# Block loads, and transposes by DMA in place of TensorE, in a fused window-attention and SwiGLU kernel

## The chip, the cores and the metric

The kernel runs on one core of a Trainium2 chip. The metric is the device time of one execution in microseconds (us). Before the change it is 247.0 us (median of three, 246.82 to 247.25). The profile is of one execution whose span is 245.4 us; all times within the kernel count from the start of that span.

## What is computed

Causal attention over a window of 128 positions plus 4 sink positions, for 4 batches, 8 heads, 768 positions and head size 64; its output, laid out as 3072 tokens of 512, goes through an RMS norm and a SwiGLU feed-forward of width 1536.

```python
keep = (pos < 4) | ((rel >= 0) & (rel < 128))     # rel = query - key
a = softmax(where(keep, q @ k.T / sqrt(64), -1e9));  x = (a @ v) as [3072, 512]
xn = x / sqrt(mean(x * x) + 1e-6) * rms_g
out = (silu(xn @ w_gate) * (xn @ w_val)) @ w_out
```

## The kernel before

**Blocks and groups.** The 3072 tokens are 24 blocks `g` of 128, six to a batch (`NT` = 6). The feed-forward takes four blocks at a time, so there are six groups `G` (group 2 is blocks 8 to 11). A block goes through a load of q, k and v (`unit_load`, L126, issued on GpSimd, with a cast to bf16), a transpose of q and k (`unit_t`, L265), scores and exponentials (`unit_s`, L399), attention times values (`unit_attend`, L488), the norm (`unit_rms`, `unit_xr`, L531 and L571) and a transpose of the normed block (`unit_x`, L602). A group then runs 12 feature tiles of gate and value products (L642) and four output products of 12 matmuls (L702).

**Two ways to transpose.** q and k of blocks 12 and up, but not of block 18, are transposed by a DMA that SyncE issues (L271); the others by TensorE (L245) with a copy by ScalarE (L279). The normed x of blocks 12 and up is transposed by DMA (L589), that of earlier blocks by TensorE (L612) with a copy by ScalarE (L621).

**Masks and sinks.** From block 8 on, GpSimd masks the exponentials (L388, L393), except in blocks that begin a batch; `pv` (L467, L471) reads them. GpSimd's queue therefore holds both loads and masks, in the order of the program. Once per batch, ScalarE copies the sink keys from the transposed k of the batch's first block (L290, `ksk`; the batches begin at blocks 0, 6, 12, 18).

**What sets the order.** A list of slots, worked off between the parts of a group (`run`, L740), writes out the order of TensorE, SyncE and GpSimd. In groups 1 to 5 parts 0 to 23 are the gate and value halves of the 12 feature tiles and parts 24 to 35 the output products; `step` (L718) puts the attention of a block at the parts in `AT` (L737) and pops its loads from `LOADS` (L738). The first group's second half has a list of its own (`FIRST`, L790), in which parts 12 to 23 are output products. The order on ScalarE and VectorE is left to a scheduler there: an instruction of theirs that waits holds all behind it.

**Buffers.** All products of TensorE rotate through eight PSUM tiles of one bank each (`psum`, L86), so a new product waits until the reader of an earlier one in its bank is done. Each GpSimd load also waits for the landing of the load eight before it. The output tiles `osb` (L707) have three buffers.

Of the kernel before, what the change touches and what calls it, by code (L numbers as in the profile page):

```python
# [15 lines left out]
P = 128  # L16
# [12 lines left out]
def kernel(  # L29
# [21 lines left out]
    NT = S // P  # L51
# [4 lines left out]
    GB = 4  # L56
# [7 lines left out]
    RMS_EPS = 1e-6 * RSQRT_SCALE ** 2  # L64
    MS_SCALE = RSQRT_SCALE / math.sqrt(DM)
    DMA_T_FROM = 12
    DMA_X_FROM = 12
    LD = 15
    FA = FTN
    POOL_MASK_FROM = 8  # L70
# [55 lines left out]
    def unit_load(g):  # L126
        if g not in QS:
            load_q(g)
            load_k(g)
        load_v(g)  # L130
# [112 lines left out]
    def transposes(ps, src, c0):  # L243
        for hp in range(HP):
            nc.tensor.transpose(  # L245
                out=ps[:, c0 + hp * P:c0 + (hp + 1) * P],
                in_=src[:, 2 * hp:2 * hp + 2, :], identity=ident,
            )
# [11 lines left out]
        )  # L260

    def by_dma(g):
        return g >= DMA_T_FROM and g != 3 * NT

    def unit_t(g):  # L265
        b, t = divmod(g, NT)
        if t == 0:
            QKT[b] = qkt.tile([P, 2, HP, S], BF16, name="qkT")
        if by_dma(g):
            for i, src in enumerate((QS.pop(g), KS_.pop(g))):  # L270
                nc.sync.dma_start_transpose(  # L271
                    out=QKT[b][:, i, :, t * P:(t + 1) * P],
                    in_=src.rearrange("p h d -> p (h d)"),
                )
            return
        ps = psum.tile([P, 512], FP32, name="pqk", tag="b1").bitcast(BF16)
        transposes(ps, QS.pop(g), 0)
        transposes(ps, KS_.pop(g), HP * P)
        nc.scalar.copy(  # L279
            out=QKT[b].rearrange("p i h s -> p (i h) s")[:, :, t * P:(t + 1) * P],  # L280
            in_=ps.rearrange("p (x c) -> p x c", c=P),
        )
# [205 lines left out]
    def unit_attend(g):  # L488

        if g % NT >= 2:  # L490
            unit_sink_av(g)
        for u in range(2):
            unit_av(g, u)
# [77 lines left out]
    def unit_xr(g):  # L571
# [14 lines left out]
        if tb == 0:  # L586
            XNT[G] = xtpool.tile([P, KTN, GN], BF16, name="xnt")
        if g >= DMA_X_FROM:
            nc.sync.dma_start_transpose(  # L589
# [5 lines left out]
    def unit_scale(gs):  # L595

        with tc.issue_after(LAST[0]):
            unit_rms(gs)
            for g in gs:
                unit_xr(g)  # L600

    def unit_x(g):  # L602
        if g >= DMA_X_FROM:
            return
        G, tb = divmod(g, GB)
        xr = XR.pop(g)
        n = KTN // 2 if g < 2 else KTN
        for k0 in range(0, KTN, n):
            ps = psum.tile([P, 512], FP32, name="pxt", tag="b1").bitcast(BF16)
            for i in range(n):  # L610
                kt = k0 + i
                nc.tensor.transpose(  # L612
                    out=ps[:, i * P:(i + 1) * P], in_=xr[:, kt * P:(kt + 1) * P],
                    identity=ident,
                )
            dest = XNT[G][:, k0:k0 + n, tb * P:(tb + 1) * P]
            src = ps[:, 0:n * P].rearrange("p (k c) -> p k c", c=P)
            if g == 2 * GB - 1:
                nc.vector.tensor_copy(out=dest, in_=src)
            elif g >= 2:  # L620
                nc.scalar.copy(out=dest, in_=src)  # L621
            elif k0 > 0:
                nc.vector.tensor_tensor(
                    out=dest, in0=src,
                    in1=gt[:, k0:k0 + n].unsqueeze(2).to_broadcast((P, n, P)),
                    op=ALU.mult,
                )
            else:
                for i in range(n):
                    nc.scalar.mul(dest[:, i, :], src[:, i, :], gt[:, k0 + i:k0 + i + 1])  # L630
# [17 lines left out]
    def parts_f(G, fts, cols, between=None):  # L648
        st = {}
        n = len(fts)  # L650

        def gate():
            st["pg"] = mms("pg", wg, G, fts, cols)
            st["th"] = spool.tile([P, 512], BF16, name="th")
            nc.scalar.activation(out=st["th"], in_=st["pg"], func=ACT.Tanh, scale=0.5)  # L655

        def val():
            pvl = mms("pvl", wv, G, fts, cols)
            p1 = spool.tile([P, 512], BF16, name="p1")
            nc.vector.scalar_tensor_tensor(  # L660
                out=p1, in0=st["th"], scalar=1.0, in1=st["pg"],
                op0=ALU.add, op1=ALU.mult,
            )
            if between:
                between()
            key = (G, fts[0] // 2)
            if key not in HT:
                HT[key] = hpool.tile([P, 2, GN], BF16, name="hT")
            i = fts[0] % 2
            LAST[0] = nc.vector.tensor_tensor(  # L670
                out=HT[key][:, i:i + n, cols],
                in0=p1.rearrange("p (n c) -> p n c", n=n),
                in1=pvl.rearrange("p (n c) -> p n c", n=n), op=ALU.mult,
            ).ins

        return [gate, val]
# [18 lines left out]
    def parts_o(G, tb):  # L695
        st = {}

        def part(i):
            if i == 0:
                st["po"] = psum.tile([P, 512], FP32, name="po", tag="b1")  # L700
            for ft in range(4 * i, 4 * i + 4):
                nc.tensor.matmul(  # L702
                    out=st["po"], lhsT=HT[(G, ft // 2)][:, ft % 2, tb * P:(tb + 1) * P],
                    rhs=wo[:, ft, :], start=(ft == 0), stop=(ft == FTN - 1),
                )
            if 4 * i + 4 == FTN:
                osb = opool.tile([P, DM], FP32, name="osb")  # L707

                nc.scalar.mul(osb, st["po"], 0.5)  # L709
                row = (G * GB + tb) * P  # L710
                n = P // 2 if G == 4 and tb < 2 else P
                for r in range(0, P, n):
                    nc.sync.dma_start(out=out[row + r:row + r + n, :], in_=osb[r:r + n])

        return [lambda i=i: part(i) for i in range(FTN // 4)]


    def step(g, p):  # L718

        b, t = divmod(g, NT)  # L720
        slots = [[] for _ in range(7)]
        if g < NB:
            if t in (2, 4):
                slots[0].append(lambda: unit_sink_scores(b, t))
            slots[0].append(lambda: unit_s(g))
            if t == 1:
                slots[2].append(lambda: unit_sink(b))
        if g <= NB:
            slots[0].append(lambda: unit_attend(g - 1))
        for n in (g + 2, g + 3):  # L730
            if n < NB and n not in (10, 12, 13) and by_dma(n) == (n == g + 3):
                slots[4].append(lambda n=n: unit_t(n))
        for n in LOADS.pop(0) if LOADS else ():
            slots[1].append(lambda n=n: unit_load(n))
        return [(p + i, u) for i, us in enumerate(slots) for u in us]

    AT = [(0, 8, 14, 20, 28), (0, 10, 18, 27)]  # L737
    LOADS = [(14, 15), (16, 17), (18, 19), (20, 21), (22, 23)]  # L738

    def run(parts, slots):  # L740

        slots = sorted(slots, key=lambda e: e[0])
        for s, f in enumerate(parts):
            while slots and slots[0][0] <= s:
                slots.pop(0)[1]()
            f()
        while slots:
            slots.pop(0)[1]()

    with tc.manual_schedule(engines=MANUAL_ALL):  # L750
# [60 lines left out]
        (19, lambda: unit_x(5)),  # L811
        (19, lambda: unit_t(9)),
        (20, lambda: unit_attend(7)),
        (18, lambda: unit_t(10)),
        (24, lambda: unit_t(12)),
        (24, lambda: unit_t(13)),
        (22, lambda: unit_sink_scores(1, 2)),
# [28 lines left out]
        ])  # L846
    with tc.manual_schedule(engines=MANUAL):

        for g in range(2 * GB + 2, 2 * GB + 6):
            FIRST.append((3 * g - 28, lambda g=g: unit_load(g)))  # L850
        for G in range(NG):
            if G == 0:
                parts, slots = fb, FIRST
            else:
                parts, slots = [], []
                for ft in range(FTN):
                    parts += parts_f(G, (ft,), slice(0, GN))
                g0, n = (9, 5) if G == 1 else (4 * G + 6, 4)
                for g in range(g0, min(g0 + n, NB + 1)):
                    slots += step(g, AT[G > 1][g - g0])  # L860
                if G + 2 <= NG:
                    gs = GROUP[GB * (G + 1)]
                    slots.append((25, lambda gs=gs: unit_scale(gs)))
                    for i, g in enumerate(gs):
                        slots.append((30 + i, lambda g=g: unit_x(g)))
            for tb in range(GB):
                parts += (parts_last if G * GB + tb == NB - 1 else parts_o)(G, tb)
            run(parts, slots)
# [33 lines left out]
```

The softmax here doesn't subtract the row's maximum and nothing guards it: scores larger than these inputs give would overflow.

## Time and profile before

| Engine | busy us | share of the span |
|---|---|---|
| TensorE, matmuls (PE) | 239.0 | 97% |
| TensorE, weight loads (PEld) | 127.8 | 52% |
| VectorE (DVE) | 163.2 | 66% |
| ScalarE (ACT) | 143.8 | 59% |
| GpSimd (POOL) | 105.3 | 43% |

The profile gives, besides these sums, a row for each group of like instructions and a timeline for each engine with start, length and, in brackets, how long the engine stood idle before and what ended that. SyncE and the DMA queues have rows for each issue, and the landing of each transfer is known. A long busy share says that an engine always has something in it; whether a change pays is read from who waits for whom in the stage that the change touches. Group 1 runs from about 66.7 to 105.5 us, group 2 from 105.5 to about 142, group 3 from there to about 178.

### The profile page before, as it was taken

What the parts mean: (1) busy time and instruction counts of PE and PEld (TensorE: products, weight loads), DVE (VectorE), ACT (ScalarE), POOL (GpSimd) and SP (SyncE); (2) the same over time, 40 slices, a digit from 0 to 9 for tenths busy, and PEclk for the clock granted to TensorE, in tenths of its full rate; (3) what the DMA queues carried; (4) which work ended last, traced back from release to release, by engine and by line L of the source; (5) the groups of instructions that cost most, each with busy time, mean ns of one, the idle gap of its engine ahead of it and who ended that gap; (6) DMA issues with size and microseconds to landing.
All of it is one profiled execution on the core that took longest, in us unless ns stands there. A gap on an engine that the chain in (4) does not pass through costs nothing.

```text
span 245.4 us, 4880 instructions
## 1 busy us (share of the span) xinstructions
PE 239.0 (97%) x1809; PEld 127.8 (52%) x1834; DVE 163.2 (66%) x367; ACT 143.8 (59%) x334; POOL 105.3 (43%) x141
## 2 busy tenths in 40 slices
PE   7999999999999999999999999999999999999995
PEld 3656888855544444554454454444444444444443
DVE  4557897878657889149778278769067885187800
ACT  2869648899977574785583385674475341323212
POOL 8967676598598997951232001233231000000000
PEclk9999999999999999999999999999999999999999
DMA  9999999999989999999001674001610002700012
GB/s 128 146 173 190 193 156 188 186 155 192 184 108 129 159 152 151 129 165 136 0 3 21 169 155 87 0 4 23 192 45 0 0 3 57 191 9 3 0 74 98
DMA packets 104937, 25.48 MB, mean 104 GB/s; under 512 B 94033, under 2 KB 101969, under 8 KB 104914
## 3 DMA queue, kind: packets, MB, share of 16 engines
q0 software_dynamic: 80704, 13.90, 75.8%
q1 hardware_dynamic: 23026, 10.95, 20.4%
q10 hardware_dynamic: 1184, 0.33, 0.6%
q8 instruction: 14, 0.23, 0.4%
q14 instruction: 9, 0.07, 0.1%
HBM read 28.31 MB, written 6.29 MB: 141 GB/s over the span
## 4 chain that ended last, share of the span: by engine, by line
PE 87%; DVE 5%; issue 3%; ACT 3%; POOL 1%; ACTq 0%; POOLq 0%
PE pg L642 24%; PE pvl L642 24%; PE po L702 22%; PE pT L411 4%; PE pv L467 2%; PE pv L471 2%; PE pw L332 2%; PE pqk L245 2%; PE po L684 1%; ACT sq L519 1%; DVE hT L670 1%; PE pv L453 1%; ACT et L420 1%; PE pT L357 1%; DVE x L508 1%
## 5 line engine op out<-in xcount | busy, mean ns | idle before, releaser
L642 PE MATMUL pg<-xnt,wg 128*128 128x512 bf16 (+1 forms) x326 | 73.6, 348 | 0.7
L642 PE MATMUL pvl<-xnt,wv 128*128 128x512 bf16 (+1 forms) x331 | 73.6, 348 | 0.2
L655 ACT ACTIVATE th<-pg 128x512 bf16<-128x512 f32 x72 | 43.2, 602 | 43.0 <-PE pg L642 41.8
L660 DVE SCALAR_TENSOR_TENSOR p<-th,pg 128x512 bf16<-128x512 bf16 x72 | 49.2, 684 | 28.1 <-ACT th L655 27.7
L702 PE MATMUL po<-wo,hT 128*128 128x512 bf16 x267 | 62.2, 379 | 0.4
L670 DVE TENSOR_TENSOR hT<-p,pvl 128x512 bf16<-128x512 bf16 x72 | 49.4, 687 | 7.8 <-PE pvl L642 1.1
L388 POOL TENSOR_SCALAR_AFFINE_SELECT et<-et 128x512 bf16<-128x512 bf16 x28 | 19.2, 694 | 70.3 <-ACT et L420 70.2
L642 PEld LDWEIGHTS <-wv 128*128 128x128 bf16 x336 | 32.4, 98 | 29.6 <-issue 0.2
L642 PEld LDWEIGHTS <-wg 128*128 128x128 bf16 x336 | 31.5, 98 | 26.5 <-issue 1.0
L420 ACT ACTIVATE et<-pT 128x512 bf16<-128x512 f32 x76 | 39.5, 609 | 4.0 <-PE pT L411 3.9
L702 PEld LDWEIGHTS <-hT 128*128 128x128 bf16 x276 | 26.1, 98 | 29.1 <-issue 0.2
L709 ACT ACTIVATE osb<-po 128x512 f32<-128x512 f32 x23 | 13.8, 598 | 31.8 <-PE po L702 27.4
L519 ACT ACTIVATE sq<-x 128x256 bf16<-128x256 bf16 x48 | 20.3, 426 | 7.9 <-DVE x L508 7.2
L121 POOL DMA_DIRECT2D v<-in_v_dram x24 | 21.8, 911 | 3.1 <-DMA wo<-in_moe_w_out_dram 2.0
L108 POOL DMA_DIRECT2D qs<-in_q_dram x23 | 20.9, 911 | 4.9 <-DMA wo<-in_moe_w_out_dram 3.0
L108 POOL DMA_DIRECT2D ks<-in_k_dram x23 | 20.9, 907 | 2.4 <-DMA wv<-in_moe_w_val_dram 0.7
L503 DVE RECIPROCAL rden<-pv 128x4 f32<-128x4 f32 x48 | 7.6, 171 | 20.3 <-PE pv L471 20.2
L508 DVE TENSOR_TENSOR x<-pv,rden 128x256 bf16<-128x256 f32 x48 | 19.9, 422 | 1.0
L582 DVE SCALAR_TENSOR_TENSOR xr<-x,y,gb 128x512 bf16<-128x512 bf16 x22 | 16.9, 814 | 0.3
L393 POOL TENSOR_SCALAR_AFFINE_SELECT et<-et 128x512 bf16<-128x512 bf16 x22 | 14.8, 673 | 0.0
L471 PE MATMUL pv<-v,et 128*128 128x65 bf16 x168 | 12.7, 194 | 0.3 <-POOL et L388 0.2
L411 PE MATMUL pT<-qkT 64*128 64x256 bf16 (+1 forms) x168 | 12.0, 262 | 0.0
(82 smaller groups left out, 192.3 us busy)
## 6 DMA issues: line engine op xcount, KB each, us to landing
out_dram<-osb SPq DMA_DIRECT2D x21, 256.0 KB, 2.4
v<-in_v_dram POOLq DMA_DIRECT2D x24, 128.0 KB, 7.2
qs<-in_q_dram POOLq DMA_DIRECT2D x23, 128.0 KB, 6.8
ks<-in_k_dram POOLq DMA_DIRECT2D x23, 128.0 KB, 6.9
wg<-in_moe_w_gate_dram POOLq DMA_DIRECT2D x6, 256.0 KB, 8.6
wv<-in_moe_w_val_dram POOLq DMA_DIRECT2D x6, 256.0 KB, 8.7
wo<-in_moe_w_out_dram POOLq DMA_DIRECT2D x2, 768.0 KB, 10.4
out_dram<-osb SPq DMA_DIRECT2D x4, 128.0 KB, 2.4
```

The costliest lines, as they stand in the source:

```text
L108: nc.gpsimd.dma_start(out=tl, in_=src[b, :, t * P:(t + 1) * P, :].rearrange("h t d -> t h d"),)
L121: nc.gpsimd.dma_start(out=V16[b][:, t, :, 0:D], in_=v[b, :, t * P:(t + 1) * P, :].rearrange("h t d -> t h d"),)
L388: nc.gpsimd.affine_select(out=ev[:, :, 0, :], in_=ev[:, :, 0, :], compare_op=ALU.is_ge, fill=0.0, base=0, pattern=[[0, x], [1, P]], channe ...
L411: nc.tensor.matmul(out=banks[u][hi][:, j * w:(j + 1) * w], lhsT=QKT[b][pr, 1, hp, t * P:(t + 1) * P], rhs=QKT[b][pr, 0, hp, t * P:t * P + ...
L420: nc.scalar.activation(out=et[:, hi].rearrange("p j n c -> p (j n c)"), in_=banks[u][hi], func=ACT.Exp, scale=inv_sqrt_d,)
L508: nc.vector.tensor_tensor(out=X16[g][:, heads_of(g, u), :], in0=pvv[:, :, 0:D], in1=RDEN.pop((g, u)).unsqueeze(2).to_broadcast((P, 4, D)), ...
L519: nc.scalar.activation(out=sq, in_=xh, func=ACT.Square, scale=MS_SCALE, accum_out=MS[g - i][:, i, u:u + 1],)
L642: nc.tensor.matmul(out=ps[:, i * n:(i + 1) * n], lhsT=w_sb[:, kt, ft * P:(ft + 1) * P], rhs=XNT[G][:, kt, cols], start=(kt == 0), stop=(kt ...
L655: nc.scalar.activation(out=st["th"], in_=st["pg"], func=ACT.Tanh, scale=0.5)
L660: nc.vector.scalar_tensor_tensor(out=p1, in0=st["th"], scalar=1.0, in1=st["pg"], op0=ALU.add, op1=ALU.mult,)
L670: LAST[0] = nc.vector.tensor_tensor(out=HT[key][:, i:i + n, cols], in0=p1.rearrange("p (n c) -> p n c", n=n), in1=pvl.rearrange("p (n c) - ...
L702: nc.tensor.matmul(out=st["po"], lhsT=HT[(G, ft // 2)][:, ft % 2, tb * P:(tb + 1) * P], rhs=wo[:, ft, :], start=(ft == 0), stop=(ft == FTN ...
```

## The change

It takes TensorE's transposes away for x of blocks 8 to 11 and for q and k of block 18 and gives them to the DMA, in the way the later blocks already have them. The loads of blocks 14 and 15 move from group 1 into the output parts of group 0, so the later loads each come a step earlier or, for 20 to 23, behind the x of the second group, so as to leave the DMA free when the x of blocks 8 to 11 is to be transposed. The transpose of block 10 stands a few instructions later, and the outputs of blocks 18 and 19 are written in halves as those of 16 and 17 are.

```diff
-    DMA_X_FROM = 12
+    DMA_X_FROM = 8
...
     def by_dma(g):
-        return g >= DMA_T_FROM and g != 3 * NT
+        return g >= DMA_T_FROM
...
-                n = P // 2 if G == 4 and tb < 2 else P
+                n = P // 2 if G == 4 else P
...
-    LOADS = [(14, 15), (16, 17), (18, 19), (20, 21), (22, 23)]
+    LOADS = [(16, 17), (18, 19), (), (), (20, 21), (22, 23)]
...
-        (18, lambda: unit_t(10)),
+        (19, lambda: unit_t(10)),
...
-        for g in range(2 * GB + 2, 2 * GB + 6):
+        for g in range(2 * GB + 2, 2 * GB + 8):
             FIRST.append((3 * g - 28, lambda g=g: unit_load(g)))
```

## Prediction

> **What bounds the kernel now.** I read the busy sums first, then TensorE's waits by stage, then the timelines of GpSimd, ScalarE and SyncE around the edits, and last the landing times of the DMAs.
>
> From the page, the busy sums and the chain that ended last, by engine:
>
> ```profile
> PE 239.0 (97%) x1809; PEld 127.8 (52%) x1834; DVE 163.2 (66%) x367; ACT 143.8 (59%) x334; POOL 105.3 (43%) x141
> ...
> PE 87%; DVE 5%; issue 3%; ACT 3%; POOL 1%; ACTq 0%; POOLq 0%
> ```
>
> TensorE is nearly always busy, and from 66.7 us on its recorded waits for other engines add up to a few tenths. So work taken off it is saved in full, and any new wait of it is lost in full: nothing later catches it up. The change is a balance of these two.
>
> GpSimd's timeline where group 0 becomes group 1, and TensorE's row that waits for it (start, length, engine, line, tiles; in brackets the idle time before and its releaser):
>
> ```profile
> 59.59 0.91 POOL L121 DMA_DIRECT2D v<-in_v_dram  x1
> 64.17 1.05 POOL L388 TENSOR_SCALAR_AFFINE_SELECT et<-et 128x512 bf16<-128x512 bf16 x1 [3.67 <-ACT et L420]
> 65.18 0.63 POOL L393 TENSOR_SCALAR_AFFINE_SELECT et<-et 128x512 bf16<-128x512 bf16 x1
> 65.77 0.63 POOL L388 TENSOR_SCALAR_AFFINE_SELECT et<-et 128x512 bf16<-128x512 bf16 x1
> ...
> 66.45 0.20 PE L471 MATMUL pv<-v,et 128*128 128x65 bf16 x1 [0.19 <-POOL et L388]
> ```
>
> GpSimd ends its last load at 60.5 and idles 3.67 us until block 8's exponentials come. TensorE takes the third mask the moment it ends: these masks have no slack.
>
> ScalarE's timeline early in group 1, and the landing times (min/median/max) of the two transposes of block 12 in front of it:
>
> ```profile
> 70.38 0.41 ACT L290 COPY ksk<-qkT 64x16 bf16<-64x16 bf16 x2 [1.11 <-DMA qkT<-ks]
> 70.82 0.60 ACT L655 ACTIVATE th<-pg 128x512 bf16<-128x512 f32 x1
> ...
> DMA to landing us min/median/max: 2.4/2.5/2.5
> ```
>
> The sink copy of batch 2 waits for that DMA, and the `th` behind it waits too, though its `pg` is ready at about 69.4. SyncE's last transposes before group 3, and the landings of the four around them:
>
> ```profile
> 108.60 1.30 SPq L271 DMA_TRANSPOSE qkT<-qs  x1
> 109.99 3.04 SPq L271 DMA_TRANSPOSE qkT<-ks  x1
> ...
> DMA to landing us min/median/max: 5.9/7.3/8.9
> ```
>
> So a transpose lands in about 2.4 us alone and in 5.9 to 8.9 us (5.5 at the least in 73 to 81 us) while loads are in flight.
>
> **What the Trainium skill says.** "DMA: Bandwidth & Descriptors", section "Issuing engines are not separate DMA queues", says that DMAs from SyncE, ScalarE and GpSimd share 16 DMA engines and interleave; the two landing times above agree. "TensorE: Matmul & The Clock Gate", in its opening table, calls the queues of ScalarE, VectorE and GpSimd strict FIFOs; the `th` held at 70.82 agrees. "PSUM — Partial Sum Buffer", "Specifications (TRN2)", gives 8 banks per partition: a late reader can be outrun by eight products, not more. The trace agrees: the two L453 matmuls of block 9, whose second waits for the `p` of feature tile 3, take 0.45 us at 74.80 against 0.27 us elsewhere. "TensorE: Matmul & The Clock Gate", "Part 4: PE-mode transpose", gives about 275 ns for a transpose in a kernel; here four of them move the next row on from 98.11 to 98.33, so I take 0.055 us each.
>
> **What is removed.** Blocks 8 to 11: 16 transposes, 16 x 0.055 = 0.9 us of TensorE; block 18: 8 x 0.055 = 0.45 us. Together -1.35 us. Six ScalarE copies go as well (four of 0.6 us, one of 1.0); nothing on TensorE waits for ScalarE's time there, so nothing. Moving block 10's transpose hides its 0.3 us wait for `ks` at 57.18, but only until TensorE waits for the masks at 66, so nothing either. The halved outputs of blocks 18 and 19: ScalarE waits 3.21 us for an output buffer at 212.69 and TensorE runs on; nothing.
>
> **Step 1, masks of block 8.** In the changed kernel's order the six loads of blocks 14 and 15 stand ahead of the masks of block 8. Six at the loads' pace of 0.87 us from 60.5 end at 65.7; the wait of each for the landing of the load eight earlier (7.0 us) adds up to 0.2. The masks start near 65.85 in place of 64.17, and the third ends 1.65 us later. Queued behind it are TensorE's `pv` of block 8 and all of group 1: +1.65 us. Bounds: 1.4 to 2.0.
>
> **Step 2, sink copy of batch 2.** SyncE issues block 12's transposes at 66.5 and 67.9 as before, but now the loads of 14 and 15 are in flight. The nearest case is block 14's pair of before, issued at 74.25 and 76.26 just as six loads had been issued: it landed with the last of these, at 81.7 and 81.95. The last load now is issued at 65.0 and lands some 7 us later, at 72; I put the k transpose at 73.0 (70.4 if alone, 75 with 7.5 us). ScalarE's queue holds `th` of tile 1 behind it. From the copy to the end of `p` of tile 3, on which the second L453 waits, it takes 74.93 - 70.38 = 4.55 us, all in VectorE's rows without a gap, and before the change this was already just the time that TensorE came. So TensorE's delay is now the copy's: 73.0 - 70.4 = 2.6 us in all, of which step 1 is a part. Call this s = 2.6; bounds 1.65 to 4.1. All of group 1 moves by s.
>
> **Step 3, x of blocks 8 to 11.** The `xr` come at 96.0 to 98.4 (+s). Four issues of 1.3 us end at 101.2 + s, and the last lands by 102.3 (2.4 us) to 104.3 (4.4, as the transpose at 69.23 with a load beside it). TensorE comes to group 2 at 105.5 - 0.9 = 104.6 + s. Hidden: nothing. The output of block 4 now goes behind them, at 101.3 + s, and the fourth output buffer waits for its landing, at 104 to 106 + s; `pg` of group 2 needs that bank at 104.6, which could cost up to 1.5 us, but step 4 takes it up.
>
> **Step 4, sink copy of batch 3.** Block 18's transposes come on SyncE behind four x, four outputs and the transposes of 16 and 17: 96.0 + 10 x 1.3 + 4 x 0.4 puts the k one at 109.4 + s, within 0.6 us of the pair shown above (109.99), with as many loads (20, 21) issued from 100 to 105.3 as 22 and 23 were then. That one landed at 115.84, so I take 116 + s; alone it would be 111.8. ScalarE's order has this copy behind the second `th` of group 2, near 108, and before the third. Behind it wait `th`, `p` and `hT` of tile 2 and after. By the eight-bank rotation the scores of block 15 need `p` of tile 2, and the next `pg` (feature tile 5) needs `p` of tile 4. With the steps seen in group 1 `p` of tile 4 ends 4.6 us after the transpose lands: 120.6 + s, where before that `pg` started at 115.41. Cost 5.2 us, in which the 0.9 us saved before it and the bank of step 3 are already contained. If alone: 111.8 + 4.6 - 115.4 = 1.0 us.
>
> **Sum.** 247.0 + 2.6 + 5.2 - 0.45 (block 18, later in group 2) = 254.35; I say 254.3 us.
>
> **Rivals.**
> - The transposes land as if alone. For it: the loads of 18 and 19 are over long before group 2, and a queue of its own might get its turn. Against: no transpose beside loads took under 4.4 us. Then 247.0 + 1.65 + 1.0 - 0.45 = 249.2 us. 20%.
> - Faster: the masks and the sink copies are hidden after all, and only TensorE's saving is left, with the 0.3 us for block 10: 247.0 - 1.35 - 0.3 = 245.35 us. For it: TensorE at 97%. Against: the mask wait at 66.45 and both copies in ScalarE's order. 8%.
> - No change: step 1 costs 1.65 us, the rest is hidden: 247.0 + 1.65 - 1.35 - 0.3 = 247.0 us. 5%.
> - Worse: block 18's transposes also wait for the loads of 22 and 23 (issued from 108.8 + s) and land 8.9 us after an issue 1 us later, at 119.2 + s, with s = 4.1: 247.0 + 4.1 + (119.2 + 4.6 - 115.4) - 0.45 = 259.05 us. 9%.
>
> **How the numbers follow.** The forecast has the rest, 58%, and reaches from about 252 (copies landing 1 us sooner in each step) to 257. The range 249.0 to 258.0 takes in the first rival and leaves out faster, no change and most of worse, some 20%. Chances: faster 0.08, same 0.05, slower 0.87.
>
> **What would show it.** Step 1: the first L388 after the loads starts near 65.9 with no idle time before it, and TensorE's `pv` waits 1.5 us or more for it. Step 2: the first L290 with a DMA as releaser waits 2 to 4 us. Step 3: `pg` of group 2 not released by a DMA. Step 4: an idle time of some 7 us ahead of the second L290, and TensorE's largest gap of the kernel at block 15. Were that copy's wait under 3 us, the forecast would be wrong; were the masks of block 8 on time, step 1 would be.

## The result, and the profile after

The changed kernel takes 265.8 us (median of four, 265.15 to 266.55) against 247.1 us for the kernel before: a ratio of 1.0758 (95% interval 1.0727 to 1.0789). The forecast was 254.3 us with a range up to 258.0: the sign was right, and the loss was more than twice the one forecast. The spans of the two profiled executions, 263.9 and 245.4 us, differ by 18.5 us, and these are followed below.

From the page of the changed kernel: the busy sums, the granted TensorE clock in 40 slices of the span (tenths of full speed, 9 for 90% or more), and the chain that ended last, by engine:

```profile
PE 241.8 (92%) x1785; PEld 127.8 (48%) x1810; DVE 162.2 (61%) x367; ACT 141.2 (54%) x329; POOL 105.0 (40%) x141
...
PEclk9999999999999999997579999999999999999999
...
PE 81%; DMA 8%; DVE 4%; ACT 3%; issue 2%; SPq 0%; DVEq 0%; ACTq 0%
```

TensorE has 24 matmul rows less and is yet busy for 2.8 us more, because some ran at a lower clock: that is the 7 and the 5 near slice 20. DMA, which before had no share in the chain that ended last, now has 8%, and TensorE's share of the span has gone from 97% to 92%.

**Step 1.** GpSimd's timeline of the changed kernel at the end of its loads, and TensorE's row that waits for it:

```profile
63.70 0.88 POOL L108 DMA_DIRECT2D qs<-in_q_dram  x1 [0.75 <-DVE y L547]
64.86 0.88 POOL L108 DMA_DIRECT2D ks<-in_k_dram  x1 [0.28 <-DVE xr L582]
65.72 0.88 POOL L121 DMA_DIRECT2D v<-in_v_dram  x1
66.60 0.66 POOL L388 TENSOR_SCALAR_AFFINE_SELECT et<-et 128x512 bf16<-128x512 bf16 x1
...
68.47 0.20 PE L471 MATMUL pv<-v,et 128*128 128x65 bf16 x1 [0.75 <-POOL et L388]
```

The masks (L388) start with no idle time, right behind the last load of block 15. TensorE takes the third one at 68.47 in place of 66.45: 2.0 us.

**Steps 2 to 4.** ScalarE's timeline: the two sink copies, and between them the last output copy of group 1:

```profile
74.78 0.41 ACT L290 COPY ksk<-qkT 64x16 bf16<-64x16 bf16 x2 [4.02 <-DMA qkT<-ks]
...
109.25 0.60 ACT L709 ACTIVATE osb<-po 128x512 f32<-128x512 f32 x1 [3.35 <-PE pv L471]
...
127.47 0.42 ACT L290 COPY ksk<-qkT 64x16 bf16<-64x16 bf16 x2 [13.63 <-DMA qkT<-ks]
```

The copy of batch 2 waits 4.0 us for a DMA (1.1 before) and that of batch 3 waits 13.6 us (none before). For the output copy at 109.25 the profile names TensorE as the releaser, but the output write issued at 105.36 lands at 109.14, just before the copy starts: it waited for the output buffer. SyncE's timeline has the transposes of block 18 and the two output writes that x pushed back:

```profile
100.14 5.12 SPq L589 DMA_TRANSPOSE xnt<-xr  x4
105.36 1.00 SPq L713 DMA_DIRECT2D out_dram<-osb  x2
...
114.64 2.19 SPq L271 DMA_TRANSPOSE qkT<-qs  x1
116.92 3.35 SPq L271 DMA_TRANSPOSE qkT<-ks  x1
```

In its records the k transpose, issued at 116.92, lands at 127.44: 10.5 us later. TensorE's timeline shows what the two waits of group 2 become there:

```profile
109.90 1.02 PE L642 MATMUL pg<-xnt,wg 128*128 128x512 bf16 x3 [0.69 <-ACT osb L709]
...
129.28 0.37 PE L411 MATMUL pT<-qkT 64*128 64x256 bf16 x1 [10.26 <-DVE p L660]
...
132.64 0.61 PE L642 MATMUL pg<-xnt,wg 128*128 128x512 bf16 x1
...
135.86 1.03 PE L642 MATMUL pg<-xnt,wg 128*128 128x512 bf16 x4
```

The last two rows are the gate matmuls of feature tiles 5 and 6. In the kernel before these were:

```profile
115.41 1.02 PE L642 MATMUL pg<-xnt,wg 128*128 128x512 bf16 x3
...
117.14 1.03 PE L642 MATMUL pg<-xnt,wg 128*128 128x512 bf16 x4
```

Last, windows of 2 us: busy time of TensorE's matmuls, its weight loads, VectorE, ScalarE and GpSimd with their counts, then the granted clock as a share of full speed, the DMA column and GB/s:

```profile
120.00:122.00 2.00, 0.00 (x0) 0.00 (x0) 0.00 (x0) 0.00 (x0) 0.00 (x0) 1.00 1.70 135
122.00:124.00 2.00, 0.00 (x0) 0.00 (x0) 0.00 (x0) 0.00 (x0) 0.00 (x0) 0.51 2.24 151
...
132.00:134.00 2.00, 1.78 (x18) 1.17 (x18) 1.72 (x6) 0.51 (x2) 0.93 (x2) 0.50 0.00 0
134.00:136.00 2.00, 2.00 (x7) 0.74 (x6) 0.69 (x1) 0.99 (x3) 0.00 (x0) 0.58 0.00 0
136.00:138.00 2.00, 2.00 (x11) 0.88 (x9) 1.07 (x2) 0.60 (x1) 0.00 (x0) 1.00 0.00 0
```

None of these engines does anything from 120 to 126 us (the window of 124 to 126, not shown, is as empty as the one before it); during it the clock falls to half, and it stays there until about 135.7, well after the matmuls are back.

The shift against the kernel before can be read off the first gate matmul (`pg`, L642) of each stage: 4.4 us at feature tile 4 of group 1 (80.08 against 75.68), 4.4 at the first of group 2 (109.90 against 105.53), 17.2 at feature tile 5 of group 2 (132.64 against 115.41), 18.7 at the tile behind it (135.86 against 117.14), and 18.5 at the end.

### The profile page after: what moved, and what is told of

Same layout as the page of the kernel before. It is cut to its first block, busy times and chain, and to the rows that moved or that the text cites. A ratio compares the mean times of both kernels' runs of the same rounds, so it can differ in the third digit from the quotient of the medians.

```text
span 263.9 us, 4849 instructions
## 1 busy us (share of the span) xinstructions
PE 241.8 (92%) x1785; PEld 127.8 (48%) x1810; DVE 162.2 (61%) x367; ACT 141.2 (54%) x329; POOL 105.0 (40%) x141
## 4 chain that ended last, share of the span: by engine, by line
PE 81%; DMA 8%; DVE 4%; ACT 3%; issue 2%; SPq 0%; DVEq 0%; ACTq 0%
PE pg L642 22%; PE pvl L642 22%; PE po L702 20%; DMA qkT<-ks 7%; PE pT L411 3%; PE pw L332 3%; PE pv L467 2%; PE pv L471 2%; DMA qs<-in_q_dram 2%; PE pqk L245 2%; DVE hT L670 1%; DVE p L660 1%; PE po L684 1%; PE pv L453 1%; PE pT L342 1%
## 5 line engine op out<-in xcount | busy, mean ns | idle before, releaser
L642 PE MATMUL pg<-xnt,wg 128*128 128x512 bf16 (+1 forms) x326 | 74.3, 350 | 1.7 <-ACT osb L709 0.7
L642 PE MATMUL pvl<-xnt,wv 128*128 128x512 bf16 (+1 forms) x331 | 74.3, 351 | 0.2
L655 ACT ACTIVATE th<-pg 128x512 bf16<-128x512 f32 x72 | 42.8, 601 | 43.3 <-PE pg L642 42.1
L388 POOL TENSOR_SCALAR_AFFINE_SELECT et<-et 128x512 bf16<-128x512 bf16 x28 | 19.3, 696 | 88.2 <-ACT et L420 88.2
L642 PEld LDWEIGHTS <-wv 128*128 128x128 bf16 x336 | 32.6, 98 | 30.2 <-issue 1.3
L642 PEld LDWEIGHTS <-wg 128*128 128x128 bf16 x336 | 31.8, 98 | 28.1 <-issue 2.6
L709 ACT ACTIVATE osb<-po 128x512 f32<-128x512 f32 x23 | 13.7, 596 | 35.0 <-PE po L702 28.4
L411 PE MATMUL pT<-qkT 64*128 64x256 bf16 (+1 forms) x168 | 13.1, 264 | 11.0 <-DVE p L660 10.5
L471 PE MATMUL pv<-v,et 128*128 128x65 bf16 x168 | 13.1, 196 | 2.2 <-POOL et L388 2.1
L411 PEld LDWEIGHTS <-qkT 64*128 64x128 bf16 x168 | 6.3, 94 | 18.0 <-issue 16.5
## 6 DMA issues: line engine op xcount, KB each, us to landing
wo<-in_moe_w_out_dram POOLq DMA_DIRECT2D x2, 768.0 KB, 11.1
```

The lines of the kernel that those rows point to most:

```text
L388: nc.gpsimd.affine_select(out=ev[:, :, 0, :], in_=ev[:, :, 0, :], compare_op=ALU.is_ge, fill=0.0, base=0, pattern=[[0, x], [1, P]], channe ...
L411: nc.tensor.matmul(out=banks[u][hi][:, j * w:(j + 1) * w], lhsT=QKT[b][pr, 1, hp, t * P:(t + 1) * P], rhs=QKT[b][pr, 0, hp, t * P:t * P + ...
L642: nc.tensor.matmul(out=ps[:, i * n:(i + 1) * n], lhsT=w_sb[:, kt, ft * P:(ft + 1) * P], rhs=XNT[G][:, kt, cols], start=(kt == 0), stop=(kt ...
```

## The experiments

**Theory A:** what costs is ScalarE's queue, which stands behind the two sink copies (L290) until a transpose by DMA has landed; how late it lands is set by the transfers around it. **Rivals:** the transfers starve the kernel whoever asks for them; the late masks make all else late; the clock's fall is a cause of its own.

### Block 18 back on TensorE

```diff
-        return g >= DMA_T_FROM
+        return g >= DMA_T_FROM and g != 3 * NT
```

> The changed kernel with q and k of block 18 back on TensorE. Theory A (ScalarE's queue stands behind the sink copy of batch 3 until block 18's k transpose lands): only the first three steps are left, so the shift of 4.4 us at tile 4 of group 1 plus 0.7 us behind the output buffer less 0.9 us of x transposes: about 251 us, and no wait of ScalarE over 2 us ahead of the second L290. Rival B (the transfers themselves, six loads and the eight transposes of x crowded around 100 to 120 us, starve the kernel, whoever asks for block 18): most of the loss stays, 258 us or more. Rival C (TensorE's clock drop is a cause of its own): the dip of the granted clock near 122 to 136 us stays although block 18 does not wait.

Measured: 252.06 us, ratio 1.0197 (1.0164 to 1.0229). Most of the loss goes with these two transposes, and the dip of the clock near 122 us too. Rivals B and C fall. Against the kernel before in the same runs (247.45 us) the loss is 4.6 us, where the terms of the expectation make 4.2. The profiled execution shows an effect that was not reckoned with, a fall of the clock at another place:

```profile
68.00:70.00 2.00, 1.25 (x11) 0.67 (x10) 1.17 (x4) 1.02 (x4) 2.00 (x5) 0.61 2.20 197
70.00:72.00 2.00, 2.00 (x6) 0.76 (x5) 0.31 (x2) 0.89 (x3) 2.00 (x4) 0.54 1.97 184
```

Behind the wait for the masks the mean clock of these windows is 0.39 and 0.46 below full speed. If the clock is either whole or at half, it was at half for 2 x (0.39 + 0.46) x 2 us = 3.4 us (an estimate), which delays TensorE by half of that. Little of it reaches the end: the copy of batch 2 waits 3.0 us for its DMA afterwards all the same, and the one execution of the four that kept the whole clock took 251.81 us, the others 251.95 to 252.82.

### The sink copies later on ScalarE's queue

The transfers stay as the change has them; only the two copies move behind the `th` (L655) that stood after them.

```diff
...
+        if b >= 2:
+            with tc.issue_after(TH[0]):     # the latest tanh, L655
+                copies()                    # the two copies of L290
...
```

> The changed kernel with all its transfers, but the two sink copies of batches 2 and 3 put later on ScalarE's queue, behind the tanhs that stood after them. Theory A (what costs is what is queued behind the copy): both waits go and with them about 2.4 us of step 2 and nearly all of step 4; step 1 (2.0 us) and the output buffer (0.7 us) stay, the transposes taken from TensorE bring 1.35 us: about 248.5 us. Rival B (the data of block 18 themselves, or crowded transfers, are what the work waits for): the wait moves to another instruction and the time stays above 258 us.

Measured: 250.36 us, ratio 1.0106 (1.0075 to 1.0136). The 12 executions part by the mean clock: five at 1.000 took 248.15 to 249.69 us, seven at 0.986 to 0.993 took 250.29 to 251.68. The five are what was expected. The others had a fall of the clock: a mean of 0.993 over 249 us is some 3.5 us at half (an estimate). Here it goes with about 2 us more, and no copy waits behind it that could hide the delay. The profiled execution is one at 1.000, so where the falls lay in the others is not shown. TensorE's only waits over 0.2 us from 60 to 140 us in the profiled execution are the two for the masks and one for an output buffer (the edit moves the lines: L479 is L471 of the other kernels, L396 is L388, L651 is L642, L719 is L709):

```profile
67.53 0.20 PE L479 MATMUL pv<-v,et 128*128 128x65 bf16 x1 [1.29 <-POOL et L396]
68.69 0.20 PE L479 MATMUL pv<-v,et 128*128 128x65 bf16 x1 [0.74 <-POOL et L396]
107.51 1.02 PE L651 MATMUL pg<-xnt,wg 128*128 128x512 bf16 x3 [0.66 <-ACT osb L719]
```

The k transpose of block 18 still lands 10.5 us after its issue here (114.47 to 124.99), and no engine waits for it. So theory A holds: of the 18.7 us some 15 come from what is queued behind two copies, the fall of the clock at block 15 included, and not from the late data themselves.

### The loads of 14 and 15 back behind the masks

```diff
-    LOADS = [(16, 17), (18, 19), (), (), (20, 21), (22, 23)]
+    LOADS = [(14, 15), (16, 17), (18, 19), (), (20, 21), (22, 23)]
...
-        for g in range(2 * GB + 2, 2 * GB + 8):
+        for g in range(2 * GB + 2, 2 * GB + 6):
```

> The changed kernel with the loads of blocks 14 and 15 back behind block 8's masks. Theory A: steps 1 and 2 go (4.4 us at tile 4 of group 1), step 4 stays because block 18's transposes still meet loads 20 to 23: about 261.5 us, with a wait of 12 to 14 us ahead of the L290 of batch 3 and about 1 us ahead of that of batch 2. Rival (the lateness of step 1 is what makes block 18's transposes late): the wait ahead of the L290 of batch 3 shrinks by the 4.4 us too, and the time falls to 257 us.

The edit also puts the loads of 16 to 19 a step later, where the kernel before has them. Measured: 260.51 us, ratio 1.0522 (1.0484 to 1.0560): 5.3 us less, in place of 4.4. The copy of batch 2 waits 1.09 us as before the change, that of batch 3 still 12 us:

```profile
122.60 0.42 ACT L290 COPY ksk<-qkT 64x16 bf16<-64x16 bf16 x2 [12.04 <-DMA qkT<-ks]
```

Step 4 does not come from the lateness of step 1.

### The loads of 22 and 23 two places later

```diff
-    LOADS = [(16, 17), (18, 19), (), (), (20, 21), (22, 23)]
+    LOADS = [(16, 17), (18, 19), (), (), (20, 21), (), (), (22, 23)]
```

> The changed kernel with the loads of blocks 22 and 23 two places later, so that of the loads only those of 20 and 21 are in flight when block 18 is transposed. Theory A1 (loads 22 and 23 set both the late issue and the late landing of block 18's k): it lands some 7 us after its issue as block 12's did and is issued 2 us earlier: 3.5 to 5.5 us less waiting, 260 to 262 us. Rival A2 (20 and 21 are enough to hold it, first come first served): landing stays within 1 us of 127.4 us and the time within 1.5 us of 265.8 us. If all the loads that stand near it were the cause and none remained, the landing would come about 2.4 us after issue, as x of blocks 8 to 11 did, and the time would be 256 us.

Measured: 261.51 us, ratio 1.0565 (1.0515 to 1.0616), as A1 had it. ScalarE's copy and SyncE's issue of that k:

```profile
124.71 0.41 ACT L290 COPY ksk<-qkT 64x16 bf16<-64x16 bf16 x2 [8.70 <-DMA qkT<-ks]
...
118.98 2.98 SPq L271 DMA_TRANSPOSE qkT<-ks  x1
```

The landing now comes 5.7 us after the issue (10.5 before), so loads 22 and 23 make up nearly half of that time. The other half of A1 missed: the issue is not earlier. At 118.98, in a trace that runs 2.2 us late at 100 us already, it stands where it stood, and still takes 3.0 us.

### TensorE kept busy during the wait

```diff
+        for _ in range(46 if g == 15 else 0):
+            nc.tensor.matmul(out=banks[0][0], lhsT=idle[:, 0:P], rhs=idle,
+                             start=True, stop=True)
```

> The changed kernel with 46 matmuls of 128x512 on idle weights added ahead of block 15's scores, where TensorE otherwise stands idle for 10 us behind block 18; they write a score bank that the real scores then overwrite, so they compute nothing that is used. At 0.22 us each they fill the idle time without lengthening it. Theory (the idle itself makes the granted clock fall to 0.5 and that costs 1.3 us between landing and tile 4 and 1.2 us after it): the wait ahead of the L290 of batch 3 stays near 13.6 us, the clock stays near 1.00 between 120 and 136 us and the time falls by about 2.5 us to 263.3 us. Rival (the clock falls for another reason, or its fall costs nothing): the time stays within 0.8 us of 265.8 us, or is longer if the added work lengthens the path.

Measured: 263.98 us (263.40 to 266.75), ratio 1.0680 (1.0605 to 1.0754): 1.8 us less than the changed kernel, with a wait of the copy that is as long as before (13.2 us). The intervals of the two ratios just overlap. The added matmuls and three windows:

```profile
119.71 10.09 PE L408 MATMUL pT<-idle 128*128 128x512 bf16 x45
```

```profile
126.00:128.00 2.00, 2.00 (x11) 0.94 (x10) 0.00 (x0) 0.00 (x0) 0.00 (x0) 1.00 1.81 127
...
130.00:132.00 2.00, 0.94 (x9) 0.29 (x5) 1.81 (x3) 2.00 (x5) 0.68 (x2) 1.00 1.47 89
...
134.00:136.00 2.00, 2.00 (x6) 0.75 (x5) 1.30 (x4) 1.39 (x5) 0.00 (x0) 0.50 0.00 0
```

With TensorE busy, the clock stays whole through the wait: the idle time is what brought it down. It falls afterwards all the same, behind the short waits at 130 to 132 us (0.53, 0.22 and 0.52 us), and that may be why only part of the 2.5 us comes back. (The profiled execution is the longest of the four, 266.75 us.)

### Each part alone, on the kernel before

```diff
-        return g >= DMA_T_FROM and g != 3 * NT      # (a) block 18 by DMA
+        return g >= DMA_T_FROM
...
-    LOADS = [(14, 15), (16, 17), (18, 19), (20, 21), (22, 23)]      # (b) the loads,
+    LOADS = [(16, 17), (18, 19), (), (), (20, 21), (22, 23)]        # and the transpose of 10
...
-        (18, lambda: unit_t(10)),
+        (19, lambda: unit_t(10)),
...
-        for g in range(2 * GB + 2, 2 * GB + 6):
+        for g in range(2 * GB + 2, 2 * GB + 8):
...
-    DMA_X_FROM = 12      # (c) x of blocks 8 to 11 by DMA
+    DMA_X_FROM = 8
```

(a) 

> The kernel before with q and k of block 18 by DMA alone; the loads stay where they are. Theory: k of 18 takes the place of block 19's transposes in the queue, issued near 110 us and landing near 115.8 us, where ScalarE comes to the copy at about 109.6 us: a wait of about 6 us ahead of the L290 of batch 3, tile 4 of group 2 5.1 us later, less 0.45 us of transposes, with up to 1.7 us more if the clock falls: 252 to 254 us. Rival (the moved loads are what makes the change slow, not block 18's transposes): within 1 us of before.

(b) 

> The kernel before with only the loads moved. Theory: steps 1 and 2, the shift of 4.4 us at tile 4 of group 1, plus up to 1.7 us in executions where the clock falls behind the idle of step 1: 251.5 to 253 us, with a wait of about 4 us ahead of the L290 of batch 2 and of less than 1 us ahead of that of batch 3. Rival (moving the loads is harmless without the other transposes): within 1 us of before.

(c) 

> The kernel before with only x of blocks 8 to 11 transposed by DMA. Theory: the sixteen transposes on TensorE are saved (0.9 us), and nothing that the path waits for stands behind: 246.5 us. Rival (here the loads of blocks 20 to 23 are in flight beside the four transposes, which the change avoided by moving them): they land 6 to 9 us after issue in place of 2.4 us, the gate matmuls of group 2 wait for them 1 to 3 us, and the time is 248 to 250 us.

| part alone | us | ratio (95%) | loss, us |
|---|---|---|---|
| (a) block 18 by DMA | 254.15 | 1.0260 (1.0206 to 1.0313) | 6.9 |
| (b) loads moved | 251.57 | 1.0154 (1.0098 to 1.0210) | 4.3 |
| (c) x by DMA | 248.82 | 1.0066 (1.0048 to 1.0084) | 1.6 |

The losses are the differences to 247.26 us, the kernel before in these runs. (a) ends just above its range, (b) at the lower end of its own. The halved outputs of blocks 18 and 19 are in none of the three; they were not run alone, but in the changed kernel TensorE has no recorded wait after 140 us. The sink copy that waits in (a), and that in (b):

```profile
115.53 0.41 ACT L290 COPY ksk<-qkT 64x16 bf16<-64x16 bf16 x2 [6.53 <-DMA qkT<-ks]
```

```profile
75.13 0.42 ACT L290 COPY ksk<-qkT 64x16 bf16<-64x16 bf16 x2 [2.97 <-DMA qkT<-ks]
```

Each part loses by itself. In (a) the k lands at 115.51, as in the order of the kernel before it was forecast to (116). In (b) the wait is 3.0 and not 4 us, but the copy is as late as in the change (75.13 against 74.78): behind a fall of the clock in this execution ScalarE came to it later. In (c) the rival was right on the time and wrong on the cause: x lands 3.5 to 5.1 us after issue, but TensorE's gate matmul waits for ScalarE, and ScalarE for an output buffer:

```profile
106.51 1.02 PE L642 MATMUL pg<-xnt,wg 128*128 128x512 bf16 x3 [1.66 <-ACT osb L709]
...
105.86 0.60 ACT L709 ACTIVATE osb<-po 128x512 f32<-128x512 f32 x1 [4.33 <-DMA out_dram<-osb]
```

The three losses add up to 12.8 us and the whole change loses 18.7. The remaining 6 us belong to no part alone.

### x by DMA with a fourth output buffer

```diff
-    opool = ctx.enter_context(tc.tile_pool(name="opool", bufs=3))
+    opool = ctx.enter_context(tc.tile_pool(name="opool", bufs=4))
...
-    DMA_X_FROM = 12
+    DMA_X_FROM = 8
```

> The kernel before with x of blocks 8 to 11 by DMA and four output buffers in place of three. Theory (with x by DMA alone, ScalarE waits 4.3 us for an output buffer because the writes stand behind the four transposes on SyncE, and the gate matmuls of group 2 wait 1.7 us for ScalarE): both waits go; the time falls from 248.8 us to between 246.4 us (all of the 0.9 us of transposes gained) and 247.3 us. Rival (the landing of x, 3.6 to 5.1 us after issue beside the loads, or the later transposes, is what costs): the time stays between 248.3 and 249.3 us.

Measured: 246.92 us, ratio 0.9983 (0.9972 to 0.9994). ScalarE's copy comes at 103.58 and TensorE's gate matmul at 104.74, with no wait:

```profile
103.58 0.60 ACT L709 ACTIVATE osb<-po 128x512 f32<-128x512 f32 x1 [1.99 <-PE po L702]
...
104.74 1.03 PE L642 MATMUL pg<-xnt,wg 128*128 128x512 bf16 x4
```

The output buffer was the whole cost of (c). 0.45 us of the 0.9 us show in the median; the interval, 0.15 to 0.7 us, does not reach 0.9.

### The change with x back on TensorE, and with two writes less

```diff
-    DMA_X_FROM = 8
+    DMA_X_FROM = 12
```

> The changed kernel with x of blocks 8 to 11 back on TensorE; loads moved and block 18 by DMA as in the change. Theory (block 18's k lands late because the loads 20 to 23 are in flight around it): a wait of 11 to 13 us ahead of the L290 of batch 3 and 263 to 265.5 us. Rival (the x transposes, and the output writes they push back on SyncE, are what makes it late): the wait falls towards the 6.5 us that block 18 by DMA alone has, and the time to 257 to 260 us.

Measured: 260.18 us, ratio 1.0518 (1.0497 to 1.0538): between the two expectations, close to the rival's.

```profile
121.92 0.41 ACT L290 COPY ksk<-qkT 64x16 bf16<-64x16 bf16 x2 [8.16 <-DMA qkT<-ks]
```

So x by DMA costs 5.6 us inside the change, where alone it costs 1.6: that is 4 of the 6 us. The others arise between the loads and block 18: this run loses 12.8 us, (a) and (b) together 11.2. On SyncE its four transposes push two output writes from 99.9 and 104.4 us to 105.4 and 106.0, among the loads of 20 and 21. The next run leaves just these two writes out, with all else in its order:

```diff
+                    if G == 1 and tb < 2:
+                        continue
                     nc.sync.dma_start(out=out[row + r:row + r + n, :], in_=osb[r:r + n])
```

> The changed kernel without the output writes of blocks 4 and 5 (0.5 MB of output left out), which on SyncE stand between the transposes of x and those of block 16. Open is why x by DMA makes block 18's k land 5.5 us later (127.4 against 121.9 us with x on TensorE). Theory (the transposes of x push these two writes from 100 to 105 us into the stretch in which six loads and the transposes of 16 to 19 are in flight, and 0.5 MB at some 185 GB/s is 2.8 us of it): the landing falls to 122 to 124.5 us, the wait ahead of the L290 of batch 3 to 9 to 11 us, and the time to 260.5 to 262.5 us, of which 0.7 us is the output buffer. Rival (the transposes of x themselves hold SyncE and the transfers behind them): landing within 1.5 us of 127.4 us and the time within 2 us of 265.8 us.

Measured: 264.09 us (260.94 to 264.80), ratio 1.0645 (1.0561 to 1.0730). The wait falls to the upper end of what was expected, but the time by only 1.7 us, which is within what the rival allowed and not clear of the noise (the two intervals just overlap):

```profile
125.52 0.42 ACT L290 COPY ksk<-qkT 64x16 bf16<-64x16 bf16 x2 [11.03 <-DMA qkT<-ks]
```

This execution ran 1.9 us late before the loads in question, after a fall of the clock at 80 us, and its records have no landing of that k; the start of the copy is taken for it. At 125.5 it lies between theory and rival. Counted from the issue of load 20's q, the k transpose lands after 23.1 us in the changed kernel (104.31 to 127.44), 19.2 us without the two writes (106.25 to 125.5) and 17.3 us with x on TensorE (104.64 to 121.90). By this count, of one execution each, the two writes are two thirds of what x adds to the landing. That is an indication and not proof; where the last 1.9 us come from is open.

### The transposes by DMA, without their waits

Built on the kernel before: x of 8 to 11 and block 18 by DMA, the later sink copies and the fourth output buffer, with the loads as before (first) or 20 to 23 one place later (second, shown; the first leaves out the edit of `LOADS`).

```diff
-    DMA_X_FROM = 12
+    DMA_X_FROM = 8
...
-        return g >= DMA_T_FROM and g != 3 * NT
+        return g >= DMA_T_FROM
...
+        if b >= 2:
+            with tc.issue_after(TH[0]):
+                copies()
...
-    opool = ctx.enter_context(tc.tile_pool(name="opool", bufs=3))
+    opool = ctx.enter_context(tc.tile_pool(name="opool", bufs=4))
...
-    LOADS = [(14, 15), (16, 17), (18, 19), (20, 21), (22, 23)]
+    LOADS = [(14, 15), (16, 17), (18, 19), (), (20, 21), (22, 23)]
```

> The kernel before with x of blocks 8 to 11 and q, k of 18 by DMA, the two sink copies of batches 2 and 3 later on ScalarE's queue, four output buffers, and the loads where they were before. Theory: no wait is left that the transposes bring, and the 1.35 us of TensorE transposes are gained: 245.9 us. Rival (some other engine takes the wait, or the idle brings the clock down): 247 to 249 us.

> As the run before it, but with the loads of 20 to 23 one place later, behind the transposes of x. Theory: x lands 2.4 us after issue in place of 4 to 5 us, but nothing waits for it, so within 0.4 us of 245.9 us. Rival (x's landing matters): faster than the run before it by over 0.4 us; if the later loads hold up block 19's transposes, slower by 1 us or more.

Measured: 246.20 us, ratio 0.9956 (0.9938 to 0.9974), and 245.99 us, ratio 0.9944 (0.9929 to 0.9960), against 247.37 us. Both beat the kernel before as well as the change. The place of the loads makes no difference that these runs can tell. The gain of the second, 1.4 us (1.0 to 1.8), is what the forecast had for the transposes taken from TensorE, 1.35 us. The later copies and the fourth buffer were not run without the transposes. In the trace of the kernel before, TensorE has no recorded wait over 0.2 us from 66 us on, so these two alone had no wait of its to take away.

## Why the prediction was wrong

The chain of waits was the forecast one in every step: masks behind loads, the rest behind the two copies. The sizes were not, and one effect was not thought of.

- **What is removed, -1.35 us.** Right in size: the last runs, which free it of its waits, gain 1.2 and 1.4 us. Five copies of ScalarE go, not six (334 rows become 329); nothing hangs on it.
- **Step 1, +1.65 us: a little small.** The masks start at 66.60, not 65.85, and the third mask's reader comes 2.0 us later, the upper bound. "The wait of each for the landing of the load eight earlier ... adds up to 0.2" was the mis-sized term: GpSimd idles 0.75 and 0.28 us ahead of q and k of block 15. The loads eight back landed at 63.14 and 64.01, and these two start 0.56 and 0.85 us later. The profile names VectorE as the releaser, but in all eight traces that have these two loads in this place the distances to the landings are 0.56 and 0.85 us, while the engine named changes from one trace to another: it is the landing that they wait for. The wait for the landing itself was about 0.2 us, as forecast; the time from a landing to the start of the load was left out.
- **Step 2, s = 2.6 us: too small.** The k transpose landed at 74.75, 6.8 us after its issue, and not at 73.0; that is close to the 75 named as the worst case, and group 1 moved by 4.4 us, just over the upper bound of 4.1. All of group 1 did move by what the copy was late, as the step said.
- **Step 3, "hidden: nothing".** x itself was hidden. The doubt named beside it, the fourth output buffer, was real: 0.7 us here, 1.7 us with x alone. Calling it "taken up" by step 4 was right, since the copy's wait is far longer; that the pushed-back writes would also make block 18's transpose land later, as the run without them indicates, was missed.
- **Step 4, 116 + s: the step that failed.** It took the landing from the pair at 109.99 of the kernel before, "with as many loads ... as 22 and 23 were then". For the old order that was right: with block 18 alone by DMA, run (a), the k landed at 115.51. In the changed order it landed at 127.44, which less s is 123.0, 7.0 us later than forecast. The loads of 22 and 23 now follow close behind those of 20 and 21, and with them issued two places later it landed 5.7 and not 10.5 us after its issue; with x back on TensorE it landed at 121.90. (These two gains overlap: together they would be more than the 7.0 us.) The issue itself was 3.1 us later than forecast: block 16's k and block 18's q took 2.60 and 2.19 us to issue in place of 1.3, and the gaps of some 0.1 us between issues were left out. The sum with its misses, all by the profiled executions:

| term | forecast | measured | miss |
|---|---|---|---|
| s | 2.6 | 4.4 | +1.8 |
| issue of block 18's k, less s | 109.4 | 112.5 | +3.1 |
| issue to landing | 6.6 | 10.5 | +3.9 |
| landing to `pg` of tile 5 | 4.6 | 5.2 | +0.6 |
| from there to the next tile: slow clock | 0 | 1.5 | +1.5 |
| to the end of the kernel | -0.45 | -0.2 | +0.2 |

The misses make 11.1 us, which is 18.5 less the 7.3 forecast, to a tenth. The forecast's 96.0 + 10 x 1.3 + 4 x 0.4 is 110.6, the end of the tenth issue; its start, 109.3, is what the 109.4 stands for. The "worse" rival, given 9%, had named the loads of 22 and 23, and the run with them later shows that they were 4.8 us of the landing; but it put the issue only 1 us later, and left the writes and the clock out (and 109.4 + 1 + 8.9 is 119.3, not 119.2).

- **The clock** was missing altogether. The forecast had an idle time of some 7 us at block 15 and costed it at its length. "TensorE: Matmul & The Clock Gate" in the Trainium skill, section "Part 1: The HAM clock gate (the "warmup" mystery)", says that the clock goes to half after an idle window of about 3.4 us and needs a busy one of that length to come back. The trace agrees, with half the clock from 122 to about 135.7 us. The run with TensorE kept busy got 1.8 us back in the median. The smaller falls differ from the page's words: one came where TensorE still worked half of the time (2.1 of 4 us busy from 66 to 70 us and no wait over 1.13 us, in the run with block 18 on TensorE). The profiled executions of the change and of the run with the later copies were busy for 1.9 and 2.0 of the same 4 us and kept the whole clock. What decides between the two is open.
- **The range** ended at 258.0 because each unknown was given its own bound from a row of the kernel before. A landing in a queue that the change itself fills is not bounded by rows in which that queue was emptier, and these misses all had one sign.

## What to carry to other kernels

When a transpose or load goes to the DMA, look first at what is queued behind its first reader on the reader's engine: here two late landings cost some 15 us through copies of 0.2 us each, and next to nothing once these copies stood later. Count the transfers that are in flight in the changed order, output writes pushed back on the issuing queue included, and not those of the old trace; and give a write its own buffer before delaying it. An idle time of TensorE of several us can cost more than its length: here the half clock behind 10 us of it made the next tile 1.5 us longer.

## What was not expected of the hardware

- The granted clock falls to half for about 3.4 us after short waits of TensorE (1.13 and 0.74 us in the run with block 18 on TensorE), in some executions and not in others of the same kernel: executions with a whole and a lower mean clock split one kernel's times into 248.15 to 249.69 and 250.29 to 251.68 us. Where a wait for a DMA came behind it, the fall cost little (251.81 against 251.95 to 252.82 us).
- The issue of a DMA transpose on SyncE, 1.2 to 1.3 us when little is in flight, took up to 3.35 us in the stretch with the most transfers in flight. The transposes of x landed 2.4 us after issue alone, and a k transpose 10.5 us after it with twelve loads and four writes around it.
- A GpSimd load that waits for the landing of the load eight before it started a fixed time after that landing: 0.56 and 0.85 us for the two loads of block 15, alike in eight traces.
